# Bias rows from one grid row, constants on ScalarE, indicators from the identity, and a pair's run in four pieces

## The chip, the core and the metric

The kernel runs on one core of a Trainium2 chip. The metric is the device time of one execution in microseconds, the median of several; the profile is of one more execution. TensorE (PE) multiplies, VectorE (DVE), ScalarE (ACT) and GpSimd (POOL) do the rest, and SyncE (SP) issues every DMA. Each engine works through its own instructions in the order in which they were written and waits on semaphores for the others.

## What is computed

Attention with a causal mask and a bias from a cumulative sum, then a gated two-layer block, for 8 batches of 8 heads, 576 positions, head size 64, model width 512, inner width 1024. Cut to what matters:

```python
def _attn_ref(q, k, v, s):
    scores = (1.0 / np.sqrt(D)) * np.matmul(q, k.transpose(0, 1, 3, 2))
    cum = np.cumsum(np.maximum(s, 0.0), axis=-1)
    bias = -(cum[:, :, :, None] - cum[:, :, None, :])
    scores = np.where(causal, -1e9, scores + np.minimum(bias, 0.0))
    attn = softmax(scores)                       # max subtracted, 1e-9 in the divisor
    return np.matmul(attn, v)

def _moe_ref(x, w_in, conv_w, w_out):            # x: heads side by side, [8, 576, 512]
    h = np.maximum(x @ w_in, 0.0)
    conv_out = sum(conv_w[k] * shifted(h, k - 1) for k in range(3))
    return (h / (1.0 + np.exp(-conv_out))) @ w_out
```

The weights arrive as 64-bit floats, which the kernel unpacks on the chip.

## The kernel before

Two heads make a **pair**, 32 pairs in all, four to a batch; both heads lie side by side on the 128 partitions. Of each pair p the program has these steps, by the names in the planner:

- qk, v: loads; hi and lo split q and k into two parts that a fast matmul can take; dr brings the pair's ten bias rows per head into a tile ek (three of these tiles take turns).
- sh (four parts, two PSUM banks each): scores for the row maxima, each with a product of ek and an indicator tile eb that adds the bias; mx takes the maxima on VectorE; tn, a "turn", transposes them on TensorE; rt copies that on ScalarE, and ds writes it into row 10 of a tile eq.
- sc (four parts, two banks each): the scores themselves, with bias and shift in one product of ek and eq; ex, the exponential, on ScalarE; mk masks on GpSimd; ad adds rows.
- sum and pv: the divisors and the product with v. Then gd, inv, ri, rb, nm divide, and xh, xl split the result for the next stage.

Of each batch, once its four pairs are done: h (matmuls with w_in, in 16 steps of twelve), re, ce, ta, ga, mu on ScalarE and VectorE, uh, ul, and o (matmuls with w_out, in 18 steps of six), evacuated by oe and stored by st. h and o use all 128 rows of the array, sh and sc use it as two halves of 64 rows, sum and pv as four strips of 32 columns.

The order on each engine is not written by hand: a planner (class Sched) plays the steps with assumed costs, taking on each engine the ready step with the lowest due time, `t.tag`, to which a long table DUE adds a correction for each step. On TensorE it prefers a step in the array's present layout. There are six PSUM banks. For pairs from B0 = 9 on, sum and pv of a pair, sc of the next and sh of the one after it form one **run** of ten steps in the order ORDER:

```python
ORDER = ("sum", "pv", "sc0", "sh0", "sc1", "sh1", "sc2", "sh2", "sc3", "sh3")
```

A run begins when all that any of its steps needs is there (`link`), and while it lasts TensorE takes nothing else.

Set-up before the first pair: from s comes the cumulative sum, its rounded part (grid) and the rest; nine rows per head, grid minus the grid at the start of one block of 64 positions, and the rest, are made in a tile bx, on VectorE and ScalarE (`bx_one`), stored to DRAM (`rows_d`) and loaded for each pair. Pairs 0 and 1 get theirs by matmuls that spread the heads' rows (gm, with selectors from `c_sel`), pair 2 straight from bx. The indicator tiles are made on GpSimd by two selects for each head (`c_masks`) and copied by ScalarE (`c_ind`, L646). The staging tiles for the weights (`open_stage`) take the place of bx once the set-up is over, and their loads wait for the stored rows.

## Time and profile before

| | us |
|---|---|
| median of 3 runs (lowest, highest) | 794.84 (794.82, 796.29) |
| the profiled execution, its own time | 793.7 |
| its span, first to last instruction | 792.0 |
| TensorE busy | 750.6 |
| VectorE busy | 562.1 |
| ScalarE busy | 436.8 |
| GpSimd busy | 334.7 |

Busy times are sums over a span with two different parts, a start of about 120 us and a steady part, so the shares tell little of either; the windows, the waits and the timelines do. A TensorE that is called busy is not a TensorE at its peak: matmuls are pipelined, and a small pause between two of them stands in no idle column.

### The profile page before, as it was taken

How to read it: one execution, taken by the hardware profiler on the slowest of the kernel's cores; microseconds unless marked ns; L12 is line 12 of the kernel's file. 1: busy time of each engine (PE TensorE's matmuls, PEld its weight loads, DVE VectorE, ACT ScalarE, POOL GpSimd, SP SyncE). 2: the span in 40 equal slices, each digit the busy share in tenths (PEclk: the TensorE clock that was granted, in tenths of full speed). 3: DMA queues.
4: the chain of work that ended last, by engine and by line, in shares of the span. 5: the costliest groups of instructions: out<-in, count | busy, mean ns of one | idle time of the engine just before them, and what ended most of it. 6: DMA issues, size and time to landing. Idle time of an engine off the chain costs nothing.

```text
span 792.0 us, 19081 instructions
## 1 busy us (share of the span) xinstructions
PE 750.6 (95%) x7536; PEld 635.2 (80%) x7536; DVE 562.1 (71%) x1357; ACT 436.8 (55%) x879; POOL 334.7 (42%) x475
## 2 busy tenths in 40 slices
PE   2788989999999999999999999999999999999998
PEld 1577778888888888888888878787787898988986
DVE  6788787855777877776778568869764878754524
ACT  4445546636564664655575546546553575555534
POOL 9136434513454455245446135534434456331211
PEclk9978989999999999999999999999999999999999
DMA  7636532220312223112122231221303311011010
GB/s 182 217 99 220 168 124 72 60 86 20 112 53 82 83 83 111 45 53 82 53 82 84 63 95 53 88 87 39 113 18 100 87 55 45 28 33 34 27 41 27
DMA packets 45322, 63.41 MB, mean 80 GB/s; under 512 B 5272, under 2 KB 30168, under 8 KB 45168
## 3 DMA queue, kind: packets, MB, share of 16 engines
q1 hardware_dynamic: 45232, 62.19, 25.3%
q8 instruction: 59, 0.97, 0.5%
q14 instruction: 31, 0.25, 0.1%
HBM read 48.69 MB, written 13.27 MB: 78 GB/s over the span
## 4 chain that ended last, share of the span: by engine, by line
PE 87%; DVE 4%; DMA 2%; ACT 2%; POOL 2%; issue 2%; SPq 0%; DVEq 0%; POOLq 0%; ACTq 0%
PE ps L1298 25%; PE ps L1425 25%; PE ps L1092 14%; PE pv L1146 11%; PE ps L996 6%; PE ps L1200 5%; ACT pt L1109 2%; DVE ad L1163 1%; DMA ht<-w_out 1%; DVE junk L1022 1%; DMA w<-w_in 0%; PE ps L1038 0%; DMA rb<-ri_d 0%; DVE r L1017 0%; POOL ad L612 0%
## 5 line engine op out<-in xcount | busy, mean ns | idle before, releaser
L1298 PE MATMUL ps<-x,wi 128*128 128x258 f32 (+1 forms) x1536 | 217.4, 299 | 0.0
L1298 PEld LDWEIGHTS ps<-x,wi 128*128 128x128 f32 x1536 | 211.2, 189 | 4.8 <-issue 0.2
L1335 DVE SCALAR_TENSOR_TENSOR ct<-ht,cw_sb,ct 128x320 f32<-128x320 f32 (+3 forms) x256 | 136.9, 539 | 82.1 <-ACT ct L1321 77.1
L1425 PE MATMUL ps<-wo,u 128*128 128x512 f32 x768 | 189.6, 398 | 0.0
L1368 POOL TENSOR_TENSOR u<-ct,u 128x512 fp32r<-128x512 f32 x64 | 85.1, 1331 | 241.9 <-ACT u L1363 219.7
L1109 ACT ACTIVATE pt<-ps,less 128x288 f32<-128x288 f32 (+1 forms) x256 | 135.4, 592 | 61.8 <-PE ps L1092 56.6
L1425 PEld LDWEIGHTS ps<-wo,u 128*128 128x128 f32 x768 | 141.0, 188 | 32.4 <-issue 0.3
L1092 PE MATMUL ps<-s 64*128 64x288 f32 (+4 forms) x1152 | 121.7, 309 | 8.2 <-ACT pt L1109 5.3
L916 POOL TENSOR_TENSOR s<-raw,s 128x1152 fp32r<-128x1152 f32 x30 | 81.7, 2724 | 60.9 <-ACT s L910 32.4
L1092 PEld LDWEIGHTS ps<-s 64*128 64x128 f32 (+1 forms) x1152 | 90.3, 179 | 18.3 <-ACT pt L1109 12.2
L1121 POOL TENSOR_SCALAR_AFFINE_SELECT pt<-pt 128x128 f32<-128x128 f32 x230 | 61.6, 294 | 91.7 <-ACT pt L1109 89.8
L1022 DVE CUSTOM_DVE_ANT_0 junk<-ps,mask 128x64 bf16<-128x64 f32 (+3 forms) x184 | 78.1, 424 | 25.7 <-PE ps L996 11.8
L1309 ACT ACTIVATE ht<-ps 128x257 f32<-128x257 f32 (+1 forms) x128 | 52.8, 412 | 78.4 <-PE ps L1298 74.1
L1146 PE MATMUL pv<-pt,v 128*32 128x448 f32 (+4 forms) x1536 | 94.6, 392 | 0.0
L1146 PEld LDWEIGHTS pv<-pt,v 128*32 128x32 f32 x1536 | 53.4, 111 | 38.7 <-issue 27.7
L996 PE MATMUL ps<-s 64*128 64x288 f32 (+4 forms) x384 | 75.4, 333 | 7.4 <-DVE r L1017 3.0
L996 PE MATMUL ps<-ek,eb 64*128 64x288 f32 (+4 forms) x384 | 68.9, 336 | 6.5 <-ACT eb L646 4.1
L1017 DVE TENSOR_REDUCE r<-ps 128x1 f32<-128x288 f32 (+4 forms) x136 | 51.2, 432 | 29.0 <-PE ps L996 29.0
L1321 ACT ACTIVATE ct<-ht,cw_sb 128x256 f32<-128x256 f32 (+1 forms) x122 | 65.4, 536 | 5.6
L1348 ACT ACTIVATE ct<-ct 128x640 f32<-128x640 f32 (+1 forms) x64 | 43.6, 682 | 41.0 <-DVE ct L1335 40.7
L996 PEld LDWEIGHTS ps<-s 64*128 64x128 f32 x384 | 52.4, 201 | 12.7 <-DVE r L1017 3.7
L1163 DVE TENSOR_TENSOR ad<-ad,pt 128x192 f32<-128x192 f32 (+2 forms) x126 | 59.9, 515 | 1.9 <-POOL pt L1121 1.6
(105 smaller groups left out, 909.2 us busy)
## 6 DMA issues: line engine op xcount, KB each, us to landing
raw<-qk SPq DMA_DIRECT2D x32, 576.0 KB
v<-vp SPq DMA_DIRECT2D x32, 320.0 KB
rb<-ri_d SPq DMA_DIRECT2D x64, 144.0 KB
out<-ob SPq DMA_DIRECT2D x32, 256.0 KB
w<-w_in SPq DMA_DIRECT2D x8, 512.0 KB
ri_d<-rs SPq DMA_DIRECT2D x32, 72.0 KB
ht<-w_out SPq DMA_DIRECT2D x8, 256.0 KB
w<-w_out SPq DMA_DIRECT2D x4, 512.0 KB
```

What stands on the lines that cost most here:

```text
L916: tt_on(e)(st[:, i, :], R_t[raw.slot][:, i], st[:, j, :].bitcast(F32), op=ALU.subtract)
L996: nc.tensor.matmul(dst[j], l, m, start=(k == 0), stop=(k == 1))
L1022: nc.vector.tensor_tensor_reduce(out=junk[:, 0 : c1 - c0], in0=bank(pb, o, o + c1 - c0), in1=mask[:, W_T[1] - w + c0 : W_T[1] - w + c1], s ...
L1092: nc.tensor.matmul(d, l, m, start=(k < 2), stop=(k >= len(steps) - 2 or (t == L and k < 2)), skip_group_check=t == L,)
L1109: nc.scalar.activation(PT_t[pts[j].slot][:, o : o + w], bank(pb, 0, w), AF.Sigmoid, bias=less, scale=0.125,)
L1146: nc.tensor.matmul(pvt[gs, o0 : o0 + c1 - c0], vt[0:jt, t, gs], PT_t[pts[g // 2].slot][0:jt, O_T[t] + c0 : O_T[t] + c1], start=(t == 0), s ...
L1163: tt_on(e)(acc, pt[:, P:S] if t == 1 else acc, pt[:, O_T[t] : O_T[t] + W_T[t]], op=ALU.add,)
L1298: nc.tensor.matmul(bank(hb, 0, XW[hf]), l, r, start=(k == 0), stop=(k == len(seq) - 1))
L1321: nc.scalar.activation(o, src, AF.Copy, scale=w)
L1335: nc.vector.scalar_tensor_tensor(cc[:, lo:hi], h_[:, sh + lo : sh + hi], cw_sb[:, 3 * f + k : 3 * f + k + 1], cc[:, lo:hi], op0=ALU.mult, ...
L1368: tt_on(e)(uu[:, 1, i, :], C_t[ct.slot][:, i, k0:hw], uu[:, 0, i, :].bitcast(F32), op=ALU.subtract)
L1425: nc.tensor.matmul(bank(pb, 0, DM), l, r, start=(fp == 0 and k == 0), stop=(fp == NF // 2 - 1 and k == len(seq) - 1),)
```

## The change

- **Bias rows.** The set-up stores the grid rows and the rest rows (`grid_d`, `rest_d`). For each pair two DMAs load one grid row nine times each, and a third the two rest rows. A new step, eq{p} in the planner (`level`), then adds to every row its constant, the negative grid value of its block, in one instruction over 74 rows and 576 columns. The constants of all pairs lie in a tile nbt, turned onto the partitions by two small matmuls (tnc). In the built program all 32 of these instructions stand on ScalarE. The rows bx, the spreading matmuls and their selectors are gone.
- **Indicators.** A table of ten columns (tab) is the sum of two pieces of the identity; each indicator tile is one ScalarE activation that repeats each column 64 times.
- **Clears** of nearly all constant tiles move from GpSimd to VectorE (`c_clear`, `c_pads`); the mask rows are made by six selects in place of eight.
- **Weights.** The staging tiles are there from the start, and their loads wait for nothing of the set-up.
- **The run in four.** ORDER has three bars. Each piece begins when its own needs are there, and between the pieces TensorE may take other steps.
- The planner's assumed price of a change of the array's layout (SWITCH) goes from 0.19 to 0.105, and the table DUE is new throughout.

A path for late pairs (`late`) is written but not built: RB is 32, the number of pairs.

```diff
-ORDER = ("sum", "pv", "sc0", "sh0", "sc1", "sh1", "sc2", "sh2", "sc3", "sh3")
+ORDER = ("sum", "pv", "sc0", "sh0", "|", "sc1", "sh1", "|", "sc2", "sh2", "|", "sc3", "sh3")
...
     "pads":
-        "0 15.84 1 -0.08 2 166.07",
+        "0 -24.77 1 321.95 2 -13.99",
...
                     if t.mode != mode:
-                        dur += 0.19
+                        dur += SWITCH
...
+    def c_clear(e):
+        nc.vector.memset(ones, 1.0)
+        nc.vector.memset(ncz, 0.0)
+        nc.vector.memset(tab[:, 0:1], 0.0)
+        nc.vector.memset(onehot, 0.0)
+        nc.vector.memset(onehot[:, 2:3], 1.0)
+        nc.vector.memset(less, -EK)
+        for r8 in R8_t:
+            nc.vector.memset(r8, 0.0)
+        nc.vector.memset(mrow, 0.0)
+        nc.vector.memset(mask, 0.0)
...
+    def c_tab(e):
+        nc.vector.tensor_tensor(
+            tab[:, 1 : NB + 2], ident[:, 0 : NB + 1], ident[:, D : D + NB + 1], op=ALU.add
+        )
+        nc.vector.tensor_tensor(unit, ident[:, 0:D], ident[:, D:P], op=ALU.add)
...
     def c_pads(i):
         def run(e):
-            eng = nc.gpsimd if e == "POOL" else nc.vector
             t = EK_t[i].bitcast(F32)
-            if i < 2:
-                t = t[:, S:FW]
-                eng.memset(t, 0.0)
...
+            nc.vector.memset(t, 0.0)
             for j in range(2):
-                eng.memset(t[D * j : D * j + NB + 1], NEG)
+                nc.vector.memset(t[D * j : D * j + NB + 2, 0:S], -1.0)
+                nc.vector.memset(t[D * j : D * j + NB + 1, S:FW], NEG)
         return run
 
     def c_ind(t):
         def run(e):
-            nc.scalar.copy(t, ind)
+            nc.scalar.activation(
+                t.rearrange("p (b c) -> p b c", c=BLK),
+                bass.AP(tab.tensor, tab.offset, [tab.ap[0], (1, NB + 1), (0, BLK)]),
+                AF.Identity, bias=tab[:, NB + 1 : NB + 2],
+            )
         return run
...
-    t_bx = [
-        add(f"bx{b}", [("ACT", 0.76), ("DVE", 0.53, True), ("POOL", 1.18, True, 0.5)], [t_cum],
-            -130 + b, bx_one(b))
-        for b in range(NB)
-    ] + [t_rest]
...
+    t_grid = add("grid", [("SP", 0.45)], [t_cum], -160, lambda e: nc.sync.dma_start(grid_d, grid),
+                 nbytes=147456)
...
-    def group(n, _=None):
-        return n if n >= B0 else None
+    def group(n, key):
+        return (n, part_of[key]) if n >= B0 else None
...
         def d_rows(e):
             for j in range(2):
-                n = 2 * p + j
-                nc.sync.dma_start(
-                    EK_t[ek.slot][D * j : D * j + NB + 1, 0:S].bitcast(F32),
-                    bx[n : n + 1].bitcast(F32) if n < DIRECT else rows_d[n],
+                src = bass.AP(grid_d.tensor, grid_d.offset + (2 * p + j) * S, [(0, NB), (1, S)])
+                nc.sync.dma_start(EK_t[ek.slot][D * j : D * j + NB, 0:S].bitcast(F32), src)
+            nc.sync.dma_start(
+                EK_t[ek.slot][NB : NB + D + 1 : D, 0:S].bitcast(F32), rest_d[2 * p : 2 * p + 2]
+            )
...
+        def level(e):
+            t = EK_t[ek.slot][0 : D + NB + 1, 0:S]
+            v, n = t.bitcast(F32), nbt[0 : D + NB + 1, p : p + 1]
+            if e == "ACT":
+                nc.scalar.activation(t, v, AF.Identity, bias=n)
+            else:
+                (nc.vector if e == "DVE" else nc.gpsimd).tensor_scalar(t, v, n, None, op0=ALU.add)
```

The built order shows where this lands. On TensorE, in the steady part, at the end of a run's second pair of steps (sc1, then sh1 with s, ek and eb, then sc2 with 448 columns), before:

```order
L1092 MATMUL ps4_69<-eq0_87,ek0_84 128x288
L1092 MATMUL ps5_70<-eq0_87,ek0_84 128x288
L996 MATMUL ps0_65<-s1_83 128x288
L996 MATMUL ps2_67<-s1_83 128x288
L996 MATMUL ps0_65<-ek1_85,eb_89 128x288
L996 MATMUL ps2_67<-ek1_85,eb_89 128x288
L1092 MATMUL ps1_66<-s0_82 128x448
L1092 MATMUL ps3_68<-s0_82 128x448
```

and now (L1109 is sc, L991 sh, L1442 o):

```order
L1109 MATMUL ps4_69<-eq0_87,ek0_84 128x288
L1109 MATMUL ps5_70<-eq0_87,ek0_84 128x288
L991 MATMUL ps0_65<-s0_82 128x288
L991 MATMUL ps2_67<-s0_82 128x288
L991 MATMUL ps0_65<-ek1_85,eb_113 128x288
L991 MATMUL ps2_67<-ek1_85,eb_113 128x288
L1442 MATMUL ps1_66<-wo_79,u3_1862 128x512 x6
L1109 MATMUL ps0_65<-s1_83 128x448
L1109 MATMUL ps2_67<-s1_83 128x448
```

Six matmuls with w_out stand where sc2 followed sh1 at once. MoE matmuls stand between two 64-row steps at 5 places of the whole program before, and at 60 now.

On VectorE, the program's first instructions, up to the cumulative chain (the scan is the third last row), before:

```order
L634 MEMSET ek1_85 128x64
L641 MEMSET ek1_85 10x64 x2
L634 MEMSET ek0_84 128x64
L641 MEMSET ek0_84 10x64 x2
L666 MEMSET pt1_93 64x576
L667 TENSOR_SCALAR pt1_93<-pt1_93 64x576
L668 SCALAR_TENSOR_TENSOR pt0_92<-pt1_93 64x576
L673 TENSOR_SCALAR big_114<-pt0_92 64x1
L674 TENSOR_SCALAR x0_94<-pt0_92,big_114 64x576
```

and now the last of 25 clears (those before it are the same five for two other bias tiles, and `c_clear`), the chain, and behind it the first instruction on a piece of w_in:

```order
L612 MEMSET ek1_85 128x640
L614 MEMSET ek1_85 11x576
L615 MEMSET ek1_85 10x64
L614 MEMSET ek1_85 11x576
L615 MEMSET ek1_85 10x64
L588 TENSOR_TENSOR v1_90<-ident_71 128x10
L591 TENSOR_TENSOR ad_96<-ident_71 128x64
L641 TENSOR_SCALAR pt1_92<-pt1_92 64x576
L642 SCALAR_TENSOR_TENSOR pt0_91<-pt1_92 64x576
L647 TENSOR_SCALAR v1_90<-pt0_91 64x1
L648 TENSOR_SCALAR pt0_91<-pt0_91,v1_90 64x576
L733 TENSOR_SCALAR w1_5122_122<-w1_10240_120 128x512
```

The chain (L641 on) stands behind the clears, and weight pieces begin right behind it; before, the first 512-column piece stood behind the maxima of two pairs.

On SP, the queue that issues all DMAs, from the store of the grid rows to the third pair's bias tile:

```order
L664 DMA grid_d_108<-pt0_91 64x576
L666 DMA rest_d_109<-pt1_92 64x576
L879 DMA raw1_81<-qk 128x1152
L884 DMA v0_89<-vp 128x640
L912 DMA ek0_84<-grid_d_108 9x576 x2
L913 DMA ek0_84<-rest_d_109 2x576
L884 DMA v1_90<-vp 128x640
L912 DMA ek1_85<-grid_d_108 9x576 x2
L913 DMA ek1_85<-rest_d_109 2x576
```

Ahead of these stand s, three loads of q and k, three pieces of w_in, the convolution's weights and two pieces of w_out; before, the first pair had no load of bias rows, and the first piece of w_in was the sixteenth row of this queue.

## Rows read from the trace of the kernel before

**Rows 1.** The page: 40 equal slices, busy tenths and granted clock.

```profile
PE   2788989999999999999999999999999999999998
PEclk9978989999999999999999999999999999999999
```

**Rows 2.** Windows: length, busy (instructions) of PE, PEld, DVE, ACT, POOL; second, PE alone.

```profile
0.00:20.00 20.00, 4.69 (x14) 3.33 (x14) 12.80 (x31) 9.68 (x15) 18.15 (x43) 1.00 0.74 180
...
119.45:788.24 668.79, 659.54 (x6326) 1.00 0.21 64
```

**Rows 3.** Timeline of the start: start, length, instruction, idle time before and its releaser.

```profile
0.82 0.59 SPq L649 DMA_DIRECT2D pt<-s  x1
2.02 0.54 DVE L666 MEMSET pt<- 64x576 f32 x1 [0.16 <-issue]
3.65 0.66 DVE L667 TENSOR_SCALAR pt<-pt 64x576 f32<-64x576 f32 x1 [1.10 <-DMA pt<-s]
18.54 1.35 ACT L646 CAST eq<-v 128x640 fp32r<-128x640 f32 x2 [4.40 <-POOL v L578]
20.57 0.61 PE L996 MATMUL ps<-ek,eb 64*128 64x288 f32 x2 [4.14 <-ACT eb L646]
```

**Rows 4.** Windows, VectorE alone, to the last maximum of pair 6.

```profile
0.00:22.00 22.00, 13.59 (x34) 1.00 0.75 179
22.00:111.83 89.83, 73.70 (x170) 0.87 0.52 171
```

**Rows 5.** Windows, TensorE alone, over the 21 whole runs: two of them, the sum.

```profile
241.66:250.46 8.80, 8.80 (x142) 1.00 0.57 177
...
552.37:564.41 12.04, 10.39 (x141) 1.00 0.34 98
...
sum 199.05, PE 190.82; mean PE 9.09
```

**Rows 6.** Timeline of TensorE: a score part that waits, a turn that waits.

```profile
473.30 0.68 PE L1092 MATMUL ps<-s 64*128 64x288 f32 x6 [0.39 <-ACT pt L1109]
...
255.76 0.27 PE L1038 MATMUL ps<-ident,r 128*32 128x128 f32 x1 [0.79 <-DVE r L1022]
```

**Rows 7.** TensorE: chain pieces of six; timeline of a part alone and within a run.

```profile
189.45 1.60 PE ps L1425 x6
...
197.61 1.40 PE ps L1425 x6
...
119.45 0.28 PE L1038 MATMUL ps<-ident,r 128*32 128x128 f32 x1
119.49 2.04 PE L1298 MATMUL ps<-x,wi 128*128 128x322 f32 x12
121.45 0.41 PE L996 MATMUL ps<-s 64*128 64x288 f32 x2
121.69 0.30 PE L996 MATMUL ps<-ek,eb 64*128 64x288 f32 x2
121.92 2.04 PE L1298 MATMUL ps<-x,wi 128*128 128x322 f32 x12
...
229.41 0.29 PE L996 MATMUL ps<-s 64*128 64x288 f32 x2
...
229.67 0.56 PE L1092 MATMUL ps<-s 64*128 64x288 f32 x6
```

**Rows 8.** VectorE groups by form: count, busy us, mean ns; idle before. A weight piece.

```profile
L770 DVE SCALAR_TENSOR_TENSOR w<-w,w 128x512 uint32<-128x512 uint32 x12 | 10.6, 885 | 0.4
...
L778 DVE SCALAR_TENSOR_TENSOR w<-w,w 128x512 f32<-128x512 f32 x12 | 8.4, 699 | 0.0
L767 DVE SCALAR_TENSOR_TENSOR w<-w,w 128x512 uint32<-128x512 uint32 x12 | 8.1, 679 | 0.0
...
L756 DVE TENSOR_SCALAR w<-w 128x512 uint32<-128x512 uint32 x12 | 5.0, 441 | 2.9 <-issue 1.3 <-DMA w<-w_in 1.1 <-DMA w<-w_out 0.4
```

**Rows 9.** ScalarE groups by form: constants added to 576 columns.

```profile
L700 ACT ACTIVATE bx<-x,ncr 64x576 fp32r<-64x576 f32 x5 | 3.4, 761 | 0.0
```

390 lines of the change are left out of this document (187 added, 203 removed), and 126 rows, old and new, of the table DUE.

## The prediction

> **What bounds the kernel now.** I read the page's slices first, then the windows, then the chain and the timelines. TensorE is busy nine tenths or more of every slice from the seventh to the last but one, and the granted clock is below nine tenths of full only in the third, fourth and sixth [rows 1]. So there are two kernels here. From 119.45 us, where the seventh pair's turn (tn of pair 6) starts [rows 7], to the last matmul at 788.24 us TensorE is busy 659.5 of 668.8 us [rows 2]: there it sets the time, and only fewer or cheaper microseconds on TensorE help. Before that point it is busy 4.7 us of the first 20 [rows 2] and waits again and again.
>
> The start: the input s lands and VectorE begins the cumulative chain at 3.65 us, but the first bias matmul waits for the indicator tile, whose source GpSimd finishes so late that ScalarE copies it from 18.54 on; TensorE gets it at 20.57 us after 4.14 us of idling [rows 3]. After that VectorE is the engine that the others wait for: busy 73.7 of 89.8 us up to the last row maximum of pair 6 at 111.83, while it was busy only 13.6 of the first 22 us [rows 4]. Its load there is row maxima and the unpacking of weights.
>
> The steady part has one visible loss. The run on a pair (sum, pv, sc0, sh0 ... sc3, sh3) may not be broken into, and needs two PSUM banks for each of its eight score parts. Of the 21 whole runs from 225 us on, twelve take 8.79 to 8.94 us; the other nine wait inside, for ScalarE's exponentials to free banks or for a VectorE sum, up to 12.04 us. All 21 take 199.05 us; 21 x 8.79 = 184.6, so the waits are 14.5 us [rows 5]. One such wait is shown [rows 6]: 0.39 us of recorded idling, though a matmul's end and its releaser's latency add to it. With 0.8 us for a turn that waited for a maximum [rows 6] the steady part has about **15.3 us** to win, not more.
>
> **The change, part by part.** *The split.* A run becomes four pieces, and MoE matmuls may stand between them. In the order of the built program MoE matmuls stand between two 64-row pieces at 60 places, where there were 5. What does such an insertion cost beyond the MoE work in it? Six matmuls of the second MoE product take 1.40 us inside a longer MoE stretch, and 1.60 when they stand alone between 64-row pieces: 0.20 more. Four 64-row score matmuls take 0.26 us, start to next start, inside a run (229.41 to 229.67), and 0.47 where MoE matmuls stand on both sides (121.45 to 121.92): 0.21 more [rows 7]. An insertion puts one more edge on each kind at either side, so it costs 0.20 + 0.21 = 0.41 us, and 55 more of them **+22.5 us**. That is a whole series of small stalls in which TensorE counts as busy; the idle column shows none of it.
>
> What it can save is the 15.3 us: with 1.4 us or more of other work between two pieces, two exponentials (about 1.2 us) have time to free their banks. I take all of it as saved, and put back **+3** for waits that stay at the boundaries where nothing is inserted (about one in four) or where ScalarE is late. Bounds for this: -4, if short waits hidden in the 8.79 go as well, and +12, if four fifths of the old waits stay.
>
> A rule bears on this. The Trainium skill (TensorEngine Tiling (Array Packing), Key Properties) states that a change of tiling mode, not just of tile, drains TensorE. By a drain alone, about half of what the rows show, the 55 insertions would cost some 11.5 us. The rows show a slow first interval after the drain too.
>
> *The start.* Removed: ten bias rows per head on VectorE and ScalarE, twelve spreading matmuls, some 9 us of indicator work on GpSimd. Added: 25 VectorE clears, three of them over whole bias tiles, now ahead of the cumulative chain. A clear of 576 columns takes 0.54 us [rows 3]; about ten are of that size and the rest near 0.1, so the chain begins at about 8.2 instead of 3.65 us. Then the grid rows go to DRAM and come back; a load of this size took 2.8 us from issue (0.82) to use (3.65) [rows 3], twice that is 5.7, and it queues behind 3 to 4 MB of weights and inputs which now come first. The bias tile is there between 17 and 20 us plus 0.8 for the constants. So the first bias matmul starts at 18 to 20.5 us: a gain of 0 to 2.5, though the indicators themselves are ready by 11. What VectorE does meanwhile matters more: three weight pieces are loaded from the first microsecond on and unpacked before the first maxima, in a stretch in which VectorE idled 8.4 us [rows 4]. A piece costs 0.44 + 0.68 + 0.89 + 0.70 = 2.7 us [rows 8], three 8.1. They leave the stretch in which the others wait for VectorE. Against it stand the clears and, from then on, waits that TensorE has of its own. In the new order a sum, a pv and a score part of pair 5 stand ahead of the seventh turn, and one MoE group of 2 us behind it. I expect the seventh turn at about 111.5 rather than 119.45 us, less those 2 us: **-6**. Bounds: 0 (the chain's delay eats it), and -14 (8.1 us at VectorE's share of 0.82 is 9.9, and 4 us of TensorE's own waits go with it).
>
> *The constants on ScalarE.* 32 activations over 576 columns; the nearest row, the block biases over 576 columns, takes 0.76 us [rows 9], so 24 us more on an engine busy 437 us of 792. Each waits for its bias tile's three DMAs, and behind it in ScalarE's order stand a turn's copy and the first MoE group's rectifier; in the built order it follows a pair's last exponentials, with three bias tiles in turn, so the load was issued microseconds before. Nothing on the path: 0; if a load is late, a MoE bank stays full for some tenths, which the +12 above holds. The third bias DMA per pair costs SP some 0.35 us of issuing each; SP waits for most of the time.
>
> **The sum.** The profiled execution took 793.7 us, 792.0 of them span. 793.7 - 6 + 22.5 - 15.3 + 3 = 797.9. The median of the runs shown is 1.1 us above the profiled execution, so the median of the changed kernel would be 798 to 799. I say 798.
>
> **The rivals.** *Faster, by the start.* VectorE's idling after 22 us is 16 us; if the early weights take most of it out, -14 instead of -6, and the hidden waits go (-4 instead of +3): 793.7 - 14 + 22.5 - 15.3 - 4 = 783; with half of each, 790. It decides from the point where the seventh turn starts before 106 us. For it: six turns in a row in which VectorE finished just ahead of TensorE; against it: the chain's later start. Chance 0.24.
>
> *Faster, by cheap switches.* Only the drain counts, since the second interval is a weight load that other orders may hide: 55 x 0.21 = 11.5, 793.7 - 6 + 11.5 - 15.3 + 3 = 787. Against it: the edges shown [rows 7] have both. This is how it would go by the Trainium skill's sentence on the drain, read strictly. Chance 0.10.
>
> *Slower still: the waits stay.* The insertions use banks too, and ScalarE has 24 us more: +12 instead of +3, 793.7 - 6 + 22.5 - 15.3 + 12 = 807. It decides where the waits at score parts sum to over 10 us. Chance 0.14.
>
> *The start gains nothing.* The later chain and the round trip through DRAM hold back the first three pairs: 0 instead of -6: 804. Chance 0.10.
>
> **How the numbers follow.** The forecast has 0.42; its own range is 793 to 803. Of it some 0.27 lies above 796.4 and most of the rest within the bound. A difference of 0.2%, 1.6 us, is about what a measurement of this kernel can tell from no change. Slower: 0.27 + 0.14 + 0.09 = 0.50. Faster: 0.24 + 0.09 = 0.33. Same: 0.17. The range reaches from 785, most of the faster cases, to 806, the edge of the waits that stay.
>
> **What would show it.** Right: 60 insertions, single MoE groups of six at 1.60 us, no idling before score parts, a seventh turn at 108 to 114 us, TensorE over 98% busy and yet a longer stretch from there to the last matmul, by 7 to 12 us. Wrong: groups of six at 1.40 to 1.50 between score parts (switches cheaper), a seventh turn before 106 (the start gave more) or after 117 (nothing), or idling at score parts of 0.3 us and more in most runs. An order in which ScalarE waits long for a bias tile would be a cause that I have priced at nothing.

## The result, and the profile after

The changed kernel takes 783.6 us (median of four runs, 781.0 to 789.2), the kernel before 795.3 on the same chip: a ratio of 0.986 (95% interval 0.983 to 0.989), 11.7 us faster. In two later series it took 786.2 and 785.3, at ratios of 0.987 both. The forecast was 798, slower, with a range of 785 to 806; the two later series lie just inside it. The direction was wrong.

The profiled execution of the changed kernel took 785.7 us, its span 783.9. Its page, against [rows 1]:

```profile
PE   0898999999999999999999999999999999999998
PEclk9998999999999999999999999999999999999999
```

TensorE fills up two slices earlier, and only the fourth slice has a granted clock of eight tenths; before, the third, fourth and sixth were under nine.

Windows of the changed kernel, TensorE alone, from the seventh turn to the last matmul, against the second line of [rows 2] (columns: stretch and length, busy, granted clock, DMA share, GB/s):

```profile
101.73:780.42 678.69, 671.75 (x6337) 1.00 0.21 64
```

The seventh turn comes at 101.73 us instead of 119.45. Both kernels have done the same TensorE work there, except for the spreading matmuls, which are gone, and for one group of twelve h matmuls (2.04 us, [rows 7]) that the kernel before had done by then. The steady part is 9.9 us longer, 2.0 of them that group; and TensorE idles 6.9 us in it instead of 9.3. So the picture of the forecast, a shorter start and a longer steady part, is what happened. The sizes weren't: the start gave more than twice what I had put down.

Timeline of its start, against [rows 3]:

```profile
10.05 0.54 DVE L641 TENSOR_SCALAR pt<-pt 64x576 f32<-64x576 f32 x1
16.23 0.67 SPq L912 DMA_DIRECT2D ek<-grid_d  x2
20.25 0.78 ACT L926 ACTIVATE ek<-ek,nbt 74x576 fp32r<-74x576 f32 x1 [4.39 <-DMA ek<-grid_d]
21.07 0.61 PE L991 MATMUL ps<-ek,eb 64*128 64x288 f32 x2 [4.89 <-ACT ek L926]
```

The chain begins at 10.05 us (25 clears ahead of it), the bias rows are asked for at 16.23, ScalarE waits 4.39 us for them and adds the constants, and the first bias matmul starts at 21.07: half a microsecond *later* than before. The gain isn't at the beginning of the start.

VectorE in the start, against [rows 4]:

```profile
0.00:22.00 22.00, 19.28 (x47) 1.00 0.80 260
22.00:101.73 79.73, 67.91 (x170) 0.96 0.50 159
```

It is busy 19.3 of the first 22 us, where it was busy 13.6. So the clears are done and the early weights unpacked where it idled.

Where the 17.7 us lie is told by the steps from one turn to the next (starts of the turns from the two timelines, TensorE alone; e2 and e16 are experiments below):

| step between turns | 1-2 | 2-3 | 3-4 | 4-5 | 5-6 | 6-7 | 1 to 7 |
|---|---|---|---|---|---|---|---|
| before | 10.8 | 15.9 | 12.4 | 17.7 | 12.8 | 23.7 | 93.3 |
| changed | 5.8 | 10.2 | 12.4 | 17.3 | 12.4 | 17.0 | 75.1 |
| e16, same start | 7.6 | 10.2 | 12.4 | 16.9 | 12.4 | 16.8 | 76.2 |
| e2, before with less unpacking | 10.7 | 15.7 | 14.7 | 16.2 | 14.4 | 17.9 | 89.7 |

Steps 3-4 and 5-6 didn't move. Three did: the first by 5 us (3 in e16), the second by 5.7, and the last by 6.7, of which the h group is 2.0. The first step differs between executions of one kernel: its 74 matmuls take 5.08 us here and 8.35 in e0, the changed kernel once more. That is most of why the seventh turn comes at 101.7 us here and at 104.6 there.

What became shorter is read from windows (TensorE alone) from the first turn to the seventh: the kernel before with two stretches of it at a low granted clock, then the changed kernel.

```profile
26.15:119.45 93.30, 82.25 (x1163) 0.87 0.49 161
39.70:49.90 10.20, 8.50 (x101) 0.50 0.34 116
73.80:80.60 6.80, 6.80 (x97) 0.50 0.73 258
```

```profile
26.65:101.73 75.08, 68.67 (x1143) 0.95 0.47 149
```

Idling falls from 11.1 to 6.4 us. The rest is busy time. In the kernel before, TensorE does 8.50, 6.80 and (the third stretch is shown below) 6.63 us of matmuls at the lower of its two clock levels (1.2 GHz). At the upper level they would take half: an estimate of 11.0 us lost. The changed kernel has one such stretch left, 6.74 us of matmuls, 3.4 us lost. Repeats agree: e14, with the start of the kernel before, loses 11.2 us so, and e0 and e15, the changed kernel again, 3.1 and 3.4. So of the 18.2 us some 7.6 are the clock, 4.7 idling, 2.0 the h group, and nearly all of the rest the first step.

### The profile page after: what moved, and what is told of

The parts are those of the page before. It is cut to its first block, busy times and chain, and to the rows that moved or that the text cites. A ratio compares the mean times of both kernels' runs of the same rounds, so it can differ in the third digit from the quotient of the medians.

```text
span 783.9 us, 19117 instructions
## 1 busy us (share of the span) xinstructions
PE 746.5 (95%) x7528; PEld 616.8 (79%) x7528; DVE 561.4 (72%) x1355; ACT 446.7 (57%) x908; POOL 334.4 (43%) x456
## 4 chain that ended last, share of the span: by engine, by line
PE 81%; DVE 7%; DMA 5%; issue 3%; ACT 2%; POOL 1%; SPq 1%; DVEq 0%; ACTq 0%; POOLq 0%
PE ps L1315 26%; PE ps L1442 25%; PE ps L1109 12%; PE pv L1163 9%; PE ps L991 6%; PE ps L1217 3%; DMA ri_d<-rs 2%; DMA rb<-ri_d 2%; DVE junk L1022 1%; DMA ht<-w_out 1%; ACT pt L1126 1%; DVE ad L1180 1%; DVE ct L1371 1%; DVE rs L1241 1%; DVE r L1013 1%
## 5 line engine op out<-in xcount | busy, mean ns | idle before, releaser
L1315 PE MATMUL ps<-x,wi 128*128 128x258 f32 (+1 forms) x1536 | 222.1, 300 | 0.9 <-ACT pt L1126 0.5
L1442 PE MATMUL ps<-wo,u 128*128 128x512 f32 x768 | 196.9, 402 | 0.5 <-ACT pt L1126 0.3
L1442 PEld LDWEIGHTS ps<-wo,u 128*128 128x128 f32 x768 | 138.6, 188 | 33.2 <-issue 3.0
L1109 PE MATMUL ps<-s 64*128 64x288 f32 (+4 forms) x1152 | 118.3, 309 | 2.0 <-ACT pt L1126 0.8
L1109 PEld LDWEIGHTS ps<-s 64*128 64x128 f32 (+1 forms) x1152 | 82.7, 177 | 25.1 <-issue 7.6
L1022 DVE CUSTOM_DVE_ANT_0 junk<-ps,mask 128x448 bf16<-128x448 f32 (+3 forms) x184 | 77.8, 423 | 29.4 <-PE ps L991 14.6
L1326 ACT ACTIVATE ht<-ps 128x257 f32<-128x257 f32 (+1 forms) x128 | 52.3, 410 | 78.5 <-PE ps L1315 75.1
L897 POOL TENSOR_TENSOR s<-raw,s 128x1152 fp32r<-128x1152 f32 x31 | 85.0, 2743 | 23.3 <-issue 13.2
L991 PE MATMUL ps<-s 64*128 64x288 f32 (+4 forms) x384 | 65.5, 319 | 10.4 <-DVE s L891 3.9
L1180 DVE TENSOR_TENSOR ad<-ad,pt 128x192 f32<-128x192 f32 (+2 forms) x131 | 63.9, 541 | 8.0 <-POOL pt L1138 7.8
L1338 ACT ACTIVATE ct<-ht,cw_sb 128x320 f32<-128x320 f32 (+1 forms) x123 | 65.6, 535 | 5.6 <-ACT ht L1326 0.4
L991 PE MATMUL ps<-ek,eb 64*128 64x288 f32 (+4 forms) x384 | 59.7, 321 | 4.9 <-ACT ek L926 4.9
L1013 DVE TENSOR_REDUCE r<-ps 128x1 f32<-128x288 f32 (+4 forms) x136 | 51.0, 431 | 18.5 <-PE ps L991 18.3
L1371 DVE TENSOR_TENSOR ct<-ct,ht 128x640 f32<-128x640 f32 (+1 forms) x64 | 53.1, 830 | 11.8 <-ACT ct L1365 11.7
```

Of the source, the lines that this page charges most:

```text
L897: tt_on(e)(st[:, i, :], R_t[raw.slot][:, i], st[:, j, :].bitcast(F32), op=ALU.subtract)
L991: nc.tensor.matmul(dst[j], l, m, start=(k == 0), stop=(k == 1 or late))
L1022: nc.vector.tensor_tensor_reduce(out=junk[:, 0 : c1 - c0], in0=bank(pb, o, o + c1 - c0), in1=add_, scale=1.0, scalar=acc if c0 else -3.0e3 ...
L1109: nc.tensor.matmul(d, l, m, start=(k < 2), stop=(k >= len(steps) - 2 or (t == L and k < 2)), skip_group_check=t == L,)
L1180: tt_on(e)(acc, pt[:, P:S] if t == 1 else acc, pt[:, O_T[t] : O_T[t] + W_T[t]], op=ALU.add,)
L1315: nc.tensor.matmul(bank(hb, 0, XW[hf]), l, r, start=(k == 0), stop=(k == len(seq) - 1))
```

## Two VectorE instructions stuck beside GpSimd, and TensorE's clock

Timeline of the kernel before (GpSimd, VectorE, TensorE), at the maxima scores (sh) that lead to the third turn, and at those that lead to the seventh:

```profile
41.05 3.02 POOL L916 TENSOR_TENSOR s<-raw,s 128x1152 fp32r<-128x1152 f32 x1 [7.44 <-DVE s L910]
41.60 3.01 DVE L770 SCALAR_TENSOR_TENSOR w<-w,w 128x512 uint32<-128x512 uint32 x1
44.54 0.81 DVE L1017 TENSOR_REDUCE r<-ps 128x1 f32<-128x288 f32 x2
45.04 0.99 PE L996 MATMUL ps<-s 64*128 64x320 f32 x2 [1.21 <-DVE r L1017]
...
101.11 2.96 POOL L916 TENSOR_TENSOR s<-raw,s 128x1152 fp32r<-128x1152 f32 x1 [5.75 <-DVE s L910]
100.88 0.69 DVE L778 SCALAR_TENSOR_TENSOR w<-w,w 128x512 f32<-128x512 f32 x1
101.48 2.87 DVE L778 SCALAR_TENSOR_TENSOR ct<-ct 128x256 f32<-128x256 f32 x1
104.27 0.81 DVE L1017 TENSOR_REDUCE r<-ps 128x1 f32<-128x288 f32 x2
104.77 0.99 PE L996 MATMUL ps<-s 64*128 64x320 f32 x2 [1.80 <-DVE r L1017]
```

L916 is GpSimd's half of splitting q and k, 3 us long. L770 and L778 are steps of a weight piece on VectorE; they take 0.69 and 0.42 us elsewhere, and here 3.01 and 2.87: each starts just after GpSimd's instruction and ends 0.55 and 0.28 us after its end. So VectorE stood still until GpSimd was through. The row maxima (L1017) stand behind that, and TensorE, which wants the PSUM banks that they read, idles 1.21 and 1.80 us. [Rows 8] had the trace of it: L770 at a mean of 885 ns beside 679 and 699 for steps of the same form. It is 692 in the changed kernel:

```profile
L747 DVE SCALAR_TENSOR_TENSOR w<-w,w 128x512 uint32<-128x512 uint32 x12 | 8.3, 692 | 0.4
```

The Trainium skill (SBUF — State Buffer, SBUF: two separate sides) has the rule: GpSimd and VectorE share a pair of ports, a VectorE instruction in a two-port mode, or with two inputs in SBUF (against a GpSimd instruction that reads SBUF, as here), takes it too; whichever starts first holds it for its whole instruction, and the other blocks. The rows agree, to the length of the wait. I hadn't weighed that rule.

What follows the second wait is dearer than the wait. Windows of the kernel before, TensorE alone:

```profile
100.00:104.50 4.50, 2.26 (x31) 1.00 0.30 79
104.50:111.40 6.90, 6.63 (x88) 0.51 0.58 202
```

TensorE is busy half of 4.5 us, and for the next 6.9 us its granted clock is 0.51, so that by the estimate above 6.63 us of matmuls do the work of 3.3.

Ahead of the third turn it is otherwise. There the clock fell at 39.7 us, before GpSimd's instruction began (41.05). Of the 5.7 us by which step 2-3 shrank, 1.6 are idling (2.7 against 1.1) and 4.1 busy time (13.2 against 9.1 for as many matmuls). The wait behind the stuck instruction is 1.21 us; whether it also kept the clock low isn't shown. In e13, where nothing sticks there, the clock is low from 38.8 to 42.2 us and the step takes 11.8 us. What made the clock fall isn't shown.

Now the changed kernel at the same place, ahead of the maxima for its seventh turn, VectorE and GpSimd:

```profile
89.89 0.69 DVE L755 SCALAR_TENSOR_TENSOR w<-w,w 128x512 f32<-128x512 f32 x1
91.29 0.76 DVE L1263 TENSOR_TENSOR rb<-pv,rb 128x576 f32<-128x576 f32 x1 [0.71 <-DMA rb<-ri_d]
91.96 0.81 DVE L1013 TENSOR_REDUCE r<-ps 128x1 f32<-128x288 f32 x2
90.11 3.00 POOL L897 TENSOR_TENSOR s<-raw,s 128x1152 fp32r<-128x1152 f32 x1 [6.37 <-issue]
```

The last step of the weight piece (L755) starts 0.22 us *ahead* of GpSimd's instruction (L897), so it takes its usual 0.69; GpSimd's takes 3.00. What VectorE does next reads PSUM and runs at its usual length. No VectorE instruction of the changed kernel is stretched by more than 0.75 us before the seventh turn; two were in the kernel before, by 4.8 us together, and each time it was one ahead of maxima that TensorE waited for.

One lower-clock stretch is left in the start of the changed kernel, from 63.6 to 70.5 us, again behind a stretch in which TensorE had little to do:

```profile
60.00:63.60 3.60, 2.28 (x24) 1.00 0.50 139
63.60:70.50 6.90, 6.74 (x89) 0.51 0.62 203
```

In the kernel before, three such stretches stand on record (39.7 to 49.9, 73.8 to 80.6, 104.5 to 111.4). In e1, an experiment below with the same start, there is none, and step 4-5 takes 14.2 us instead of 17.3: about 3 us for one stretch.

## The experiments

All compare with the kernel before on the same chip, whose medians were 795.2 to 796.1 us.

| | us | ratio (95%) | seventh turn |
|---|---|---|---|
| e0, changed kernel again | 786.2 | 0.987 (0.984, 0.991) | 104.6 |
| e1, runs made whole | 870.1 | 1.093 (1.084, 1.101) | 98.8 |
| e2, before, less unpacking | 792.0 | 0.995 (0.993, 0.997) | 116.2 |
| e3, late weights | 791.4 | 0.995 (0.993, 0.997) | 108.5 |
| e4, clears on GpSimd | 787.8 | 0.990 (0.986, 0.994) | 103.9 |
| e5, no bars, planned anew | 826.0 | 1.036 (1.032, 1.041) | 104.4 |
| e6, before, idle matmuls | 793.2 | 0.998 (0.996, 1.000) | 119.8 |
| e7, bias rows first | 785.6 | 0.987 (0.984, 0.990) | 104.8 |
| e8, new start, whole runs | 836.5 | 1.050 (1.047, 1.054) | 121.9 |
| e9, old start, split runs | 828.1 | 1.040 (1.038, 1.043) | 130.6 |
| e10, changed, idle matmuls | 786.6 | 0.989 (0.986, 0.992) | 103.9 |
| e11, bias rows and maxima first | 792.3 | 0.995 (0.993, 0.997) | 110.5 |
| e12, whole runs in the first half | 782.7 | 0.983 (0.979, 0.988) | 104.2 |
| e13, new start, then before | 782.8 | 0.984 (0.981, 0.987) | 104.7 |
| e14, before with constants | 796.1 | 1.001 (0.998, 1.003) | 119.5 |
| e15, changed, side by side | 785.3 | 0.987 (0.985, 0.989) | 104.5 |
| e16, kernel of e13 | 783.1 | 0.984 (0.982, 0.986) | 102.8 |
| e17, kernel of e12 | 783.6 | 0.984 (0.982, 0.986) | 104.3 |

The seventh turn at 101.73 us, in the first profiled execution of the changed kernel, is its earliest; its two repeats have 104.6 and 104.5.

### Is it the start? New start, and then the order of the kernel before

Three kernels that joined whole runs to the new start came out far slower than either parent. **e1** takes the MoE steps out of the runs of the changed kernel and puts them behind their run; **e5** takes the bars away and lets the planner plan anew; **e8** has the changed kernel's order to the seventh turn and from there, on every engine, that of the kernel before, with PSUM banks given out anew. **e9** is the reverse of e8.

```diff
@@ e5 @@
-ORDER = ("sum", "pv", "sc0", "sh0", "|", "sc1", "sh1", "|", "sc2", "sh2", "|", "sc3", "sh3")
+ORDER = ("sum", "pv", "sc0", "sh0", "sc1", "sh1", "sc2", "sh2", "sc3", "sh3")
@@ e1 @@
+            elif t.eng == "PE" and gap not in KEEP:
+                inner.append(t)
...
+            new = put_off(order, some, steps[-1])
@@ e8 and, from the kernel before, e9 @@
+    new = order[: order.index(by["tn6"])]
...
+    for n in REST_ORDER.split():
```

> The changed kernel with its order kept, but with the MoE matmuls taken out of the runs and put right behind them (51 of 60 steps; the other nine find no free bank there). The start up to the seventh turn is untouched. Theory (the split costs more than it saves): in the trace of the changed kernel a group of six alone takes 1.60 instead of 1.40 us and the four pieces of a pair take 8.95 instead of 8.79 us, so an insertion costs 0.25 us; some 46 fewer of them give back 11.5 us; the waits in the runs come back from about 6 to 14.5 us. Sum -3: about 780.5 us, the stretch from the seventh turn to the last matmul 675 instead of 678.7 us. Rival (the split is where the gain comes from): the waits come back in full in every run and the time goes above 787 us. Rival 2 (insertions are dear, as predicted, at 0.41 us): -19 + 8.5, 773 us.

> The changed kernel with the three bars taken out of ORDER, planned anew: a run is again one piece, and the order of every engine is fitted to that. Up to the first run (pair 9) the order is that of the changed kernel word for word; MoE matmuls stand between two 64-row steps at 9 places instead of 63. Theory (the split costs more than it saves, as in the prediction): the stretch from the seventh turn to the last matmul is back near the 668.8 us of the kernel before (plus 2 us for a MoE group that moved), 671 instead of 678.7, and the total near 777 us. Rival (the split pays, as its waits would be longer than those it replaces): that stretch takes 679 us or more, the total 784 us or more.

> The changed kernel with two orders joined: every engine's order up to the seventh turn is the changed kernel's, and from there on the kernel before's, with whole runs (steps already done are skipped, the constants step of each later pair is put on ScalarE ahead of the run before it, and 49 steps wait a few places for a buffer). Here the steady part is one that was planned for whole runs, unlike in the run without bars. Theory (as predicted, the steady part with the split is the slower of the two by about 8 us): from the seventh turn to the last matmul 670 to 672 instead of 677 to 679 us, the total 776 to 780 us on a chip where the changed kernel takes 784 to 786. Rival (the steady part is not worse for the split; the difference lies in what the start left over): the total is 784 us or more.

> The other half of the same cross: the kernel before up to the seventh turn, and from there on the order of the changed kernel, with the run in four (without its constants step, which this kernel does not have). Theory: the start is that of the kernel before, seventh turn at 119 us, the rest 676 to 680 us instead of 668.8, the total about 803 us. Rival (the split pays): 795 us or less.

All four came out slow, with TensorE idle 35 us (e5) and 53 us (e1) behind the seventh turn. Waits of TensorE in e5, 200 to 700 us (who waits for what: sum, times, longest):

```profile
PE ps L1109 <- ACT pt L1126: 10.3, 32, 0.8
```

Either whole runs can't live with the constants step that ScalarE now has, or these four only broke the fit between the engines. Two kernels told these apart. **e14** is the kernel before with one ScalarE step more for each of 22 pairs:

```diff
+                    ek_ = EK_t[load_of[f"dr{p}"].alloc[0].slot][0 : D + NB + 1, 0:S]
+                    nc.scalar.activation(ek_, ek_.bitcast(F32), AF.Identity)
```

> The kernel before, with one more ScalarE step for each of pairs 10 to 31: zero added over the 74 rows and 576 columns of the pair's bias tile (the result is the same), in the place where the changed kernel adds its constants. It measures by itself what the constants cost a kernel with whole runs. 22 steps of about 0.76 us: if ScalarE has room, 0 to +2 us and no new idling before score parts. If whole runs cannot live with the step (the explanation for the three slow kernels in which whole runs stood in the new order), TensorE's idling before score parts grows and the time rises by 8 us or more.

Same time (0.998 to 1.003). The step's row, by line and form, and TensorE's longest sum of waits from 200 to 700 us:

```profile
L1504 ACT ACTIVATE ek<-ek 74x576 fp32r<-74x576 f32 x22 | 15.0, 681 | 2.3 <-DMA ek<-rows_d 2.2
...
PE ps L1092 <- ACT pt L1109: 4.3, 12, 0.4
```

15 us more on ScalarE, and the wait for its exponentials is 4.3 us where it was 4.2. **e13** has the changed kernel's order up to the sum of pair 7 and then the order of the kernel before on all engines, with *its* PSUM banks; the constants stay on ScalarE.

```diff
+    new = order[: order.index(by["sum7"])]
...
+            by[n].eng = e
+            new.append(by[n])
+            old.update(zip(by[n].alloc, map(int, banks)))
```

> The changed kernel up to the sum of pair 7, then every engine in the order of the kernel before to the end: whole runs, with their banks. The constants step stays on ScalarE, right behind a pair's last exponential. Nothing is left out. By the traces at equal progress the steady part behind that point should take what it took in the kernel before, so that the median is 776 to 780 us (the lead of 15.6 us at sum 7 is kept). If the whole runs need what the constants step on ScalarE takes away, idling before score parts grows pair by pair and the median is over 790 us.

782.8 us. Its whole runs repeat those of the kernel before one by one: windows over a run without and one with waits, first of e13, then of the kernel before (the windows of [rows 5] end a little earlier, so these are cut alike):

```profile
232.20:241.07 8.87, 8.87 (x142) 1.00 0.55 176
542.49:554.63 12.14, 10.48 (x142) 1.00 0.33 98
```

```profile
241.66:250.53 8.87, 8.87 (x142) 1.00 0.57 176
552.37:564.48 12.11, 10.46 (x142) 1.00 0.34 99
```

Over the same 22 runs that makes 210.5 us in both. So the constants cost a kernel with whole runs nothing, and the start alone, without any split, is worth the whole gain. What e1, e5, e8 and e9 show is how tightly the steps on all engines are fitted to each other; e8 loses 17 us at its join already (seventh turn at 121.9), and its banks were given out anew; which of the two makes the rest of its 50 us isn't told.

### What does the split do?

**e12** has whole runs from the sum of pair 7 to that of pair 19 and the four pieces from there on. It, e13 and the changed kernel then ran side by side in more rounds: **e15** (the changed kernel), **e16** (e13's kernel), **e17** (e12's kernel). e12's edit is e13's, with another list of steps.

> The changed kernel, except that from the sum of pair 7 to the sum of pair 19 every engine takes its steps in the order of the kernel before, with whole runs and their PSUM banks; behind that the changed kernel's order, with the run in four pieces. Nothing of the computation is left out. If the split loses some 8.7 us in that stretch because the runs waited little there (the two traces at equal progress), the stretch becomes that much shorter and the median is 777 to 781 us. Rival, the run in four is needed by the constants step on ScalarE, which whole runs have to wait for: idling before score parts grows, and the time is 788 us or more. Second rival, only the joins cost: the loss stands in the first two or three pairs behind sum 7 and behind sum 19, and between them the turns follow each other as in the kernel before.

> The changed kernel, beside e16 and e17 on one chip, in more rounds: 785.5 us (the median of its eight runs so far).

> The kernel of e13 (new start, then whole runs in the order of the kernel before). It differs from e15 in the split and its order alone. If the split costs what the two profiled executions show from the seventh turn on (678.7 against 674.2 us), the median is 2 to 5 us under that of e15. If the split only trades waits for insertions, it is within 1.5 us of e15; if the split wins, as its authors' order may have been fitted to do, it is over by more.

> The kernel of e12 (whole runs from sum 7 to sum 19, the split behind). If the split loses in the first half and breaks even in the second, this is the fastest of the three, 1 to 4 us under e15 and at or up to 2 us under e16. If the split's gain and loss lie everywhere alike, it lies between the two.

785.3 us (784.4 to 786.5) with the split against 783.1 (782.0 to 783.6) without, 783.6 (781.3 to 784.8) with half of it. The split, with the order that goes with it, costs 2.2 us; the hybrid lies between, and isn't told from e16. So e16, the change without its split, is 2 us faster than the change.

Where these 2 us come from is read from the two profiled executions, from the seventh turn to the last matmul (from each matmul's start to the next one's, idle time apart, summed by the step that it belongs to):

| us | h | o | sum, pv | sc, sh | turns | idle | all |
|---|---|---|---|---|---|---|---|
| e15, split | 214.6 | 212.3 | 96.7 | 146.5 | 1.2 | 4.5 | 675.8 |
| e16, whole | 211.1 | 205.4 | 98.3 | 147.2 | 1.4 | 10.1 | 673.5 |

The MoE matmuls, the same number in both, take 10.4 us more when they stand between the pieces: 55 insertions, **0.19 us** each. The 64-row steps take nothing more. And the split saves 5.6 us of idling, 1.6 in sum and pv, and 0.9 in the other steps; these 2.5 us count as busy, and that they are short waits isn't shown. Waits of TensorE from 200 to 700 us, e16 and then e15:

```profile
PE ps L1495 <- ACT pt L1512: 4.2, 12, 0.4
PE ps L1603 <- DVE ad L1566: 1.5, 3, 0.7
```

```profile
PE ps L1109 <- ACT pt L1126: 0.7, 2, 0.3
PE ps L1217 <- DVE ad L1180: 0.4, 1, 0.4
```

Twelve waits for exponentials became two, as the change means it, and three for a sum became one. Now the price. The chain of the changed kernel, two o groups of six, one alone between score parts and one within a longer MoE stretch:

```profile
477.01 1.59 PE ps L1442 x6
514.46 1.40 PE ps L1442 x6
```

And a run of four pieces, as windows (TensorE alone):

```profile
555.21:559.58 4.37, 4.37 (x82) 1.00 0.07 23
561.15:562.14 0.99, 0.99 (x13) 1.00 0.32 102
565.90:567.76 1.86, 1.86 (x25) 1.00 0.00 0
569.35:571.07 1.72, 1.72 (x25) 1.00 0.00 0
sum 8.94, PE 8.94; mean PE 2.23
```

The group alone costs 0.19 us more, as [rows 7] had it. The four pieces of this run together take 8.94 us where a whole run takes 8.87: 0.07 for three cuts, not 0.21 for each.

### What in the start is worth what?

**e2** leaves out three of the four unpacking instructions of four weight pieces in the kernel before, 9.1 us of VectorE's work (the line stands in two functions).

```diff
+                if name in ("wo4.0", "wo5.0", "wi5", "wi6"):
+                    return
```

> The kernel before, with the second and third unpacking step left out for four weight pieces that lie between the first and the seventh turn (so these weights are wrong in the output): 2.27 us of VectorE each, 9.1 us in all. Theory (VectorE alone sets the time up to the seventh turn): the seventh turn moves from 119.45 to 110 us or earlier, and the total from 795.3 to about 786 us; where TensorE idles less, its clock falls less often and 2 to 4 us more are won. Rival (TensorE's own waits and its low clock set it): the seventh turn moves by less than 4 us, the total stays above 791 us.

It gains 4 us, 3.3 of them by the seventh turn: taking VectorE's load away does little by itself. But one of the instructions left out is the L778 that stood right ahead of the stuck one (100.88 above). The one that stuck, here L782, now starts 0.23 us ahead of GpSimd's and takes 0.42, so e2 shows that place without the collision. Its timeline there (GpSimd, VectorE), and its windows (TensorE) over the same stretch as above:

```profile
103.24 2.72 POOL L920 TENSOR_TENSOR s<-raw,s 128x1152 fp32r<-128x1152 f32 x1 [7.52 <-DVE s L914]
103.01 0.42 DVE L782 SCALAR_TENSOR_TENSOR ct<-ct 128x256 f32<-128x256 f32 x1
103.85 0.82 DVE L1021 TENSOR_REDUCE r<-ps 128x1 f32<-128x288 f32 x2 [0.42 <-PE ps L1000]
```

```profile
100.00:104.50 4.50, 3.80 (x65) 1.00 0.40 122
104.50:111.40 6.90, 6.90 (x136) 1.00 0.61 209
```

The maxima follow at once, TensorE doesn't wait, and the clock stays at its upper level. From the restart of TensorE (the first sh matmul for the seventh turn, behind a wait for VectorE's split) to the seventh turn e2 takes 103.24 to 116.17, 12.9 us; the kernel before takes 101.11 to 119.45, 18.3, and e14, which has the same collision, 102.46 to 119.53, 17.1. So one collision with what followed it cost **4.1 to 5.4 us**: 1.80 and 1.95 of idling, and the same 220 matmuls busy for 16.5 and 15.1 us instead of 12.9. e2 gave part of that back: it has lower-clock stretches of its own at 60.6 and 91.4 us, and steps 3-4 and 5-6 are about 2 us longer. What the collision ahead of the third turn cost isn't isolated: there was no run that took only that one away.

**e3** puts the loads of three w_in pieces behind the store of the bias rows; **e7** sets the first tasks in another order, so that the bias rows come first; **e11** does the same and puts the first pieces' unpacking behind the next pairs' maxima; **e4** clears two of the three bias tiles on GpSimd and puts two loads of w_out behind the stores.

```diff
@@ e3 @@
+MOVED = ("wi6", "wi7", "wi2")
+BEHIND = "rst"
@@ e7 @@
+FIRST = """pads0 ident s qk1 qk0 clear wi7 tab cum hi1 ind0 eb pads1 tri mrow lo1.0 hi0 ncr grid rest tnc nbt ind1 rst
...
@@ e11, besides @@
+        ("wi31 wi11 wi01", "mx2.1.1.0"), ("wi21", "mx1.1.1.0"), ("wi61", "mx0.1.1.0"), ("wi1 wi3 wi0", "ds0"),
...
@@ e4 @@
-            nc.vector.memset(t, 0.0)
+            eng = nc.gpsimd if i else nc.vector
+            eng.memset(t, 0.0)
```

> The changed kernel with one part undone: the loads of the first three pieces of w_in stand in SP's queue behind the stores of the grid and rest rows, as the weight loads did before, and their VectorE steps come later by as much. Theory (the early weights are what made the start shorter): some 8 us of unpacking move into the stretch in which VectorE is waited for, the seventh turn goes from 101.7 to about 109 us and the total from 783.6 to about 791 us. Rival (that stretch got shorter because other pieces were put off beyond the seventh turn, and early loading gives little): less than 3 us, below 787 us.

> The changed kernel with its first 45 steps in another order: the cumulative chain right behind the first clears, two bias tiles cleared on GpSimd, and in SP's queue the stores of grid and rest and the first pair's bias load ahead of two weight pieces, the later loads of q and k and v. Theory (the whole program is shifted by the first bias matmul, as the late weights showed: first bias matmul 6.2 us later, seventh turn 6.8 later): the first bias matmul comes at about 16.5 instead of 21.07 us, the seventh turn 3 to 4.5 us earlier, the total 779 to 781 us. Rival (the unpacking of weights, now later, comes into the stretch that waits for VectorE): the gain is gone by the third turn.

> As the run with the bias first (there the first bias matmul came 7.9 us earlier, at 13.75 us, but the first turn no earlier, since three weight pieces stood ahead of the first maxima on VectorE): now two of these pieces stand behind the first maxima and others behind the next ones, and the loads of the next pieces behind the first row stores. Theory (from the first turn on TensorE sets the pace, VectorE has room for the pieces later): the first turn comes at 19 to 21 instead of 27.2 us, the seventh at 97 to 100 instead of 104.6, the total 5 to 7 us below the changed kernel. Rival (VectorE sets the pace over the whole start): the gain is gone by the seventh turn.

> The changed kernel with the clears of two of the three bias tiles on GpSimd instead of VectorE (3.8 us off VectorE ahead of the cumulative chain), and two loads of w_out put behind the stores of the grid and rest rows in SP's queue. Theory (VectorE sets the start from its first clear on): the chain begins at about 6 instead of 10.05 us, the first bias matmul at 17 to 19 instead of 21.07, every turn up to the seventh comes 2.5 to 4 us earlier, and the total is 780 us. Rival (GpSimd is now late with the low part of q and k, or TensorE waits for the loads): the first turn gains less than 1 us and the total stays within 2 us of 783.6.

In e3 the first turn is 6 us late (32.85), and from there to the seventh it takes 75.6 us, in the changed kernel 75.1 to 77.9: what was won between the turns stays, and the late first turn costs the total some 6 us (0.995 of the kernel before against 0.987). e7 brings the first bias matmul to 13.75 us from 21.07, and the first turn still stands at 27.09, since VectorE unpacks three pieces ahead of the first maxima: no gain. e11 also turns that round, has its first turn at 21.43 us, 5.8 ahead of e0's, and its seventh at 110.5, 5.9 behind e0's. Of the 11.7 us that it loses between the two, 5.75 are one wait of TensorE (1.0 in e0) for ScalarE's split of q and k, which stands behind a late load of w_out (timeline, TensorE and ScalarE):

```profile
37.61 0.61 PE L1098 MATMUL ps<-s 64*128 64x288 f32 x2 [5.75 <-ACT s L998]
35.49 0.43 ACT L847 ACTIVATE ct<-ht 128x256 f32<-128x256 f32 x1 [3.55 <-DMA ht<-w_out]
```

Besides, three lower-clock stretches come back, and an unpacking step sticks beside GpSimd again (1.79 instead of 0.69 us at 50.81). So e11 doesn't tell what unpacking *before* the first maxima is worth; e3 puts the early loading at some 6 us, in an order in which the first maxima stand behind the unpacking. e4 starts the chain at 4.78 us and gains nothing either: by e7 an earlier chain wins nothing in this order, and half of e4's lead is lost in the same way as above. Timeline, VectorE and GpSimd:

```profile
7.30 2.77 DVE L714 TENSOR_SCALAR pt<-pt,v 64x576 f32<-64x576 f32 x1
7.15 2.61 POOL L963 TENSOR_TENSOR s<-raw,s 128x1152 fp32r<-128x1152 f32 x1
```

The rounding of the sums, 0.57 us in the changed kernel, waits here behind a GpSimd instruction.

**e6** and **e10** put idle matmuls into TensorE's waits, 37 in the kernel before and 45 in the changed one, to see whether the lower clock can be kept off so.

```diff
@@ e6 @@
+    warm_at = {"tn0": 11, "sh2.0": 8, "sc0.3": 7, "sh1.0": 3, "sh1.2": 8}
...
@@ e10 @@
+    warm_at = {"tnc": 28, "sh0.0": 10, "tn0": 1, "sc0.1": 2, "sh2.0": 4}
```

> The kernel before, with 37 idle matmuls of 256 columns, in five groups, in TensorE's pauses between 24.6 and 45 us (into the bank of pv, which nothing uses there); the work is unchanged. Theory (a TensorE that pauses runs at half clock afterwards, and this is most of what the start of the changed kernel gets rid of): the stretch at half clock from 39.7 to 49.9 us goes, the third turn comes at 48 to 49 instead of 52.9 us, and the total falls by 3 to 5 us to about 791. Rival (VectorE sets the pace, TensorE's clock only fills its pauses): the clock stays at full speed and the third turn moves by less than 1 us.

> The changed kernel with 45 idle matmuls of 128 columns (fp32, all 128 rows) in TensorE's pauses before and around the first bias matmul and turn, into the bank of pv, which is free there; the work is unchanged. In the trace of the kernel before the first two pairs' matmuls take 0.44 us where they take 0.29 later, and full clock is on record only from 36.3 us on; in the changed kernel from 26.1 us in one profiled execution and from 35.3 in another. Theory (TensorE at its granted clock sets the start from the first turn on): with full clock from 20 us or earlier the second turn comes at 32 instead of 35.5 us, the seventh at 99 to 102 instead of 104.6, the total 2 to 5 us below the changed kernel. Rival (VectorE sets it): the first two matmul groups are shorter but every turn stays within 1 us.

e6 gains 2 us at most, with its seventh turn no earlier; e10 gains nothing against e0. The lower-clock stretches stayed. **e0** is the changed kernel once more.

> The changed kernel itself, for comparison on the same chip: 781 to 789 us, with no stretch of half clock or one of 7 us ahead of the seventh turn; every theory expects the same of it.

786.2 us, seventh turn at 104.6, with one stretch at the lower clock, 66.0 to 72.8 us, as in the first profiled execution.

## Why the prediction was wrong, point by point

- **The start, -6: the step that failed.** Its measure is e16, which has the new start and whole runs: 12.9 us below the kernel before in the medians. At the seventh turn the changed kernel's three profiled executions are 14.9 to 17.7 us ahead, 12.8 to 15.7 without the h group. The forecast had the seventh turn at 111.5; it came at 101.7 to 104.6. Three errors in it. I took the later chain and the round trip through DRAM as a cost that eats the gain; they do hold back the first bias matmul (21.07 us, I had 18 to 20.5), but e7 brings it to 13.75 and gains nothing. I counted the early unpacking as 8.1 us of VectorE work moved, and took off most of what that is worth; e3 puts the early loading at some 6 us. And I had no term for TensorE's clock, though [rows 1] showed three slices under nine tenths: by the estimate above it cost 11.0 us up to the seventh turn and now costs 3.4, the largest part of the gain. One piece of that has a cause that a run isolates: the stuck instruction ahead of the seventh turn, 4.1 to 5.4 us with the lower clock behind it. I saw neither collision, though [rows 8] showed the other one, a step of 885 ns among its like of 680 to 700. Why the clock fell in the other two stretches, and why only one is left, stays open.
- **The insertions, +22.5: mis-sized, measured +10.4.** The 0.20 us on the side of the 128-row matmuls held (0.19). The 0.21 on the 64-row side was read from one part with MoE on both sides [rows 7] and added for each insertion; over a run of four pieces it comes to 0.02. I should have compared whole pieces with a whole run, not one edge with one interval. The rival by the Trainium skill's sentence on the drain (TensorEngine Tiling (Array Packing), Key Properties), which I had priced at 11.5 us from half of the same rows, was nearer.
- **The waits, -15.3 + 3: mis-sized, measured -8.1.** 5.6 of idle and 2.5 that had counted as busy. Of the waits that are left, those for exponentials are few, as I thought.
- **The constants on ScalarE, 0: right** (e14: 0.998 to 1.003; the step takes 0.776 us, I had 0.76). So was a longer steady part: +7.9 us without the h group in the first profiled execution against 10.2 forecast, by two errors that nearly cancel; but the three executions of the changed kernel differ by 2.5 us there, and part of it isn't the split's. e16 too takes 3.0 us longer than the kernel before behind the seventh turn, without a split (673.8 against 668.8 + 2.0), and its lead at the runs from pair 8 on is some 3 us less than at the seventh turn. By the sums of the steps it is 1.8 us in sc and sh, 0.8 of idling and 0.5 in the turns; why, I haven't found.
- **The rivals.** "Faster, by the start" had the right part, the right test (a seventh turn before 106 us) and 783 us. The number is luck: it kept +22.5 for the insertions and took off 19.3 for the waits, where 10.4 and 8.1 were measured. Nor is its reason borne out, that VectorE's idling goes: of 16.1 us from 22 us on [rows 4], 11.8 are left. It had 0.24, because I weighed against it a delayed chain that decides nothing in this order. "Cheap switches" was right too, at 0.10. That both could hold together, and most of the sum with them, I had not priced.

Put together with what was measured: the kernel before at 796.0, start -12.9, insertions +10.4, waits -8.1 gives 785.4; e15 measured 785.3. This only says that medians and profiles agree: the first of these terms is e16's own difference, and the other two are the difference of the profiled executions of e15 and e16.

## What to carry to other kernels

When one engine is the bottleneck of a stretch, look in the groups by form for a mean that stands out among its like, and in the timeline for the single long instruction behind it: beside a long GpSimd instruction a VectorE one may take four to seven times its length, and what waits behind it pays more than that. A reordering removes or makes such collisions, so compare the order of *two* engines around every wait, not of one. Count the busy time at the lower clock beside the idle time. Price a cut in a run by whole pieces against the whole run, and before asking what a split saves, see how many of its parts wait at all.

## What I had not expected of the hardware

- TensorE's granted clock fell although it was kept busy. Windows of e6, with idle matmuls in the waits:

```profile
32.80:39.60 6.80, 5.96 (x82) 1.00 0.39 131
39.60:49.90 10.30, 10.16 (x118) 0.50 0.37 115
```

  5.96 us of 6.80 busy, and the lower level for the next 10.3 us. The busy column doesn't tell when it falls.
- The two stuck VectorE instructions come at the same place in every profiled execution of the kernel before's start (e14: 3.02 us at 40.68 and 2.86 at 102.83; e6: 3.00 and 2.86; e9: 3.02 and 2.86): no accident of one run, but a property of the order. e2, with its steps left out ahead of the second, has the first alone.
